# A transformer block on one core: the first loads in one queue in the order of need, the fourth q group behind k^T v, another priority table

## The chip, the cores and the metric

The kernel runs on one core of one Trainium2 chip. The metric is device time in microseconds (us) of that core, the median of several runs; less is better. One further execution was recorded by the hardware profiler, and all times of single instructions are from it.

The engines go by these names: PE is TensorE (matmuls; PEld its weight loads), DVE is VectorE, ACT is ScalarE, POOL is GpSimd, SP is SyncE. SP, ACT and POOL also start DMAs.

## The reference

The input x has 2048 rows (tokens) of 512, in bf16. Cut to what matters:

```python
phi = lambda t: jnp.where(t > 0, t + 1, jnp.exp(t)) + 1e-06

def A(x, wqkv, wo):                       # 32 heads of 16
    q, k, v = split(x @ wqkv)
    pq, pk = phi(q), phi(k)
    kv  = pk^T v                          # one 16x16 matrix for each head
    z   = sum of pk over the tokens
    o   = (pq @ kv) / (pq @ z + 1e-06)
    return o @ wo

def B(x, w_in, w_sp, b_sp, w_out):        # w_in 512x1792, w_sp 2048x2048, w_out 896x512
    z  = gelu(x @ w_in)
    z1 = z[..., :896]
    z2 = layernorm(z[..., 896:])
    g  = w_sp @ z2 + b_sp[:, None]        # mixes the tokens
    return (z1 * g) @ w_out

h  = x + A(layernorm(x), wqkv, wo)
h2 = h + B(layernorm(h), w_in, w_sp, b_sp, w_out)
```

Layer normalisation has no weights: it subtracts the mean of a row and divides by the root of the variance plus 1e-5.

## The kernel before

The 2048 rows are 16 tiles of 128 rows; two tiles are a pair, and four tiles (512 rows) are a group. Everything stays in on-chip memory from the first load to the last store.

**Stages.** (1) Each tile of x gets its statistics on DVE (L607, L611), ACT works out the reciprocal root (L621, L623), and DVE writes the normalised tile xn (L635). The statistics of several tiles share one pair of ACT instructions: the groups are 0, 1, 2-3, 4-7, 8-11, 12-15 (`LN1`). Four buffers hold xn. (2) xn is transposed to xT, either on TensorE (L673) with an ACT copy out of PSUM (L678), or by a DMA transpose that SP issues (L662); the constant `XDMA` says from which pair on DMA does it. (3) For each pair k and v are projected (L705: eight matmuls of 128x512 for k, eight for v). k goes through phi: Exp on ACT (L684) and two DVE instructions (L685, L692). v is copied by ACT (L719). (4) q is projected transposed, for each group in two halves of eight matmuls (L731), each with its phi. (5) k^T v is accumulated over all 16 tiles (L754, 64 narrow matmuls), masked to the heads and transposed on DVE (L766, L772, L774), and multiplied with wo (L784, L789, L792). (6) The denominators come from matmuls of q with the sums of k (`den`, L804; Ln and Exp on ACT, L808 and L811), are spread over the columns (`spread_den`, L821, L827) and scale q (`scale_pq`, L843, L847). (7) The scaled q times the product of stage 5 is added to x (L876, L881), and that is h. (8) h is normalised and transposed again, z2 (L904) and z1 (L949) are projected, and Gelu runs on ACT (L913, L954). (9) w_sp, which DMA transposes (L553) have brought in transposed, mixes the tokens (L979), and w_out projects the result (L997), which is stored.

**Order.** No engine's order is written by hand. `Program.op` records each operation with a cost and a priority; `schedule` then runs a list planner over the five engines. At each step it takes, on the engine that can start first, the candidate that can start at once (or within `PATIENCE`) with the lowest priority number. The order that comes out is fixed for each engine, and semaphore waits are put in for what an operation depends on. A dependency in `deps` becomes a wait; one in `after` only holds the planner back. The table `NUDGE` adds a number to each operation's priority, in the order in which operations are recorded. The planner counts 0.5 us of SP's time for a load, 1.3 us for a DMA transpose, and for the data of all loads one common wire of 340 GB/s.

**First loads.** SP issues x tile 0, the k weights in two halves, and seven pairs of x (x2 to x8, 256 KB each). ACT issues x tile 1 and the v weights; POOL issues the q weights, and later wo, w_in and w_out, each of which waits until POOL's DMA before it has landed. Behind its loads SP has the 16 DMA transposes for the first quarter of w_sp and ten for the second, with priority 5000, so that the transposes of xn go first wherever the planner has them ready.

**q groups.** `NQ1` says how many of the four q groups get priority `Q0 - 5 + gq` (75 and up). The others, none before the change, get `Q0 + Q3P` (88); k^T v has `Q0 + 2` (82).

```python
for gq in range(NQ1):
    for f in (0, 2):
        o = q_proj(gq, f, Q0 - 5 + gq)
load("pool", "wout", wout.all(), B_w_out.rearrange("(c p) f -> p c f", p=P), FH * D * 2).deps[o] = True
...
for gq in range(NQ1, NG):
    for f in (0, 2):
        q_proj(gq, f, Q0 + Q3P)
```

Of the kernel before, what the change touches and what calls it, by code (L numbers as in the profile page):

```python
# [10 lines left out]
P = 128  # L11
# [98 lines left out]
class Program:  # L110
# [13 lines left out]
    def op(self, eng, cost, fn, r=(), w=(), prio=None, after=(), dma=None, nbytes=0, lag=0.0):  # L124
        o = Op()
        o.eng, o.fn, o.cost, o.seq = eng, fn, cost, len(self.ops)
        o.prio = o.seq if prio is None else prio
        o.after, o.deps, o.tiles = list(after), {}, []
        o.marked, o.sem, o.semval, o.grp, o.bytes, o.lag = False, None, None, dma, nbytes, lag
        o.raw = set()  # L130
        for x in list(r) + list(w):
            t = getattr(x, "tile", None)
            if t is not None and t not in o.tiles:
                o.tiles.append(t)
                t.ops.append(o)
        rk = [k for x in r for k in x.keys]
        wk = [k for x in w for k in x.keys]
        for k in rk:
            p = self.writer.get(k)
            if p is not None:  # L140
                o.deps[p] = True
                o.raw.add(p)
        for k in wk:
            p = self.writer.get(k)
            if p is not None:
                o.deps[p] = True
                o.raw.add(p)
            for q in self.readers.get(k, ()):
                if q is not o:
                    o.deps[q] = True  # L150
        for k in rk:
            self.readers.setdefault(k, []).append(o)
        for k in wk:
            self.writer[k] = o
            self.readers[k] = []
        self.ops.append(o)
        return o
# [213 lines left out]

NUDGE = [
    0, 0, 0, 0, 0, 0, 0, 0, 0, 0, 0, 0, 0, 0, 0, 0, 0, 0, 0, 0, 0, 0, 0, 0, 0, 0, 0, 0, 0, 0, 0, 0, 0, 0, 0, 0,
    0, 0, 0, 0, 0, 0, 0, 0, 0, 0, 0, 0, 0, 0, 0, 0, 0, 0, 0, 0, 0, 0, 0, 0, 0, -24.5, 27.5, -1.5, 28, -65,
    396.5, 122.5, 93.5, 46, -45.5, -424.5, -26.5, -342, 3.5, 6.5, 17, -91, -52, -53.5, 190, -89, -15, 63.5,
    18.5, 5, -20, -57.5, -9, 143, 6.5, 0, -8, -3.5, 105.5, 89.5, 1122, -12, -84, 78.5, -154.5, 9, 512, -147.5,
    -5.5, -30.5, -26.5, 57, 2321.5, 66.5, 2453.5, 101, 2881.5, 445, 2436, -29.5, -0.5, 170.5, 126.5, 14.5, -4.5,
    -181.5, 53, -54, 0.5, 0, -1, -36.5, 79, 980, -17, 8, 29.5, 182.5, 0, 0, -61.5, 49, -72.5, -307.5, 112,
    191.5, -14, 0, -265, 0, -60.5, -64, 24, 154.5, -27, 112.5, 48, -217.5, 9, -9.5, 116, -88.5, 85.5, 182.5,
    -15.5, -45, 384, 113.5, 51.5, 69, 94.5, 14, 133.5, 521.5, 113.5, -157, 50.5, 391, -44.5, 116.5, -37, 404,  # L380
    274, 70.5, 62, -308, -114.5, 0, 366.5, 276.5, 195, 70.5, 61, -64, 53.5, -93, -104.5, -16, 0, -29, 0, 2, 9.5,
    40.5, 60.5, 133.5, 237, -64, -20, 173.5, 21, -26.5, -14.5, 26, 43, 655, 3377, 107.5, 92, 106, 226, 157,
    -173, 247.5, 64.5, 408.5, 11.5, -47, 85.5, -26, 112.5, 223.5, 8.5, -101.5, -48, -143.5, -44, -89, 0, 0,
    -141.5, -45, -54.5, 26, -11.5, -11.5, -364, 666, 25.5, -58, -73, -164, 0, 21.5, 0, 104.5, 73.5, 511.5, 151,
    258.5, 1, 1, 92, 51.5, 120, -98, 31, -100.5, 54, -130.5, 43, -2, -10.5, 34, 69.5, -53, 60.5, 11, -10.5,
    32.5, 295, 92.5, -9, 0, -83.5, 19.5, -118.5, 0, -10, 112, -15, -24.5, 5.5, 1.5, -119.5, -119.5, -54.5,
    -412.5, 83, -16.5, 72.5, 82, -46.5, 96.5, 944.5, 0, 55.5, 0, 300.5, -15, 745.5, 199.5, 311, 0, 147.5, -1,
    73, -49.5, -152, 12.5, 64.5, -567, 73.5, 15, 92.5, 136, 150.5, 7, 20, 126, 155.5, 807.5, -246, -154.5,
    -33.5, 1.5, 321, 14, 6, 99, 163, -11, 359, -28.5, -578.5, 0, -4.5, -371, -125.5, -205.5, -105, -58.5, -7, 0,
    448.5, 322, 6.5, 59, 5, 1, -1.5, 123.5, 45, 36.5, 36.5, -80, -8.5, 66, 10, 26, 1146.5, 186, 281.5, 31, 13,  # L390
    133, 13.5, -16.5, 67.5, 340, 428, 104, 213.5, -0.5, -1.5, 56, -261, -1.5, -1.5, 10, -63, -38.5, -28.5, -4,
    -6.5, -146.5, -342, 78.5, -66, 82.5, -333, -702, -291, 117.5, -20.5, 1205.5, 16, 54, 65, -31.5, -83.5,
    -68.5, -86.5, -178, -24, -279, -228.5, -63.5, -72.5, -44.5, 9.5, 75, 63.5, 157, -66.5, -47, 670.5, 83, 91.5,
    156.5, 458.5, -59, 218, 123, 39.5, 0, -53.5, 0, 98.5, -73.5, 60, -6, 33, -62, -73, -61.5, -4.5, 36.5, 183.5,
    -23.5, -11.5, 198, -21.5, 37, -173, -11.5, -49.5, -1, 130.5, 220.5, -7.5, -223.5, -16.5, -11, -20, -85.5,
    -21, 0, 5, -9.5, -18.5, -42.5, -80.5, -1.5, 20.5, -66.5, -62.5, 0.5, 1.5, 37.5, -10, 83.5, -614.5, -4.5,
    -567, 4, -52, 95, -286, -101.5, 27, 41.5, 13, 78, 241.5, -182.5, -39.5, 45.5, 7.5, 87.5, 3, -72.5, -124,
    -352, -11, -72, -9, -61, -104, 16.5, -210, 131.5, 36, 36.5, 49, -61.5, -14.5, 215, 186.5, -88.5, -113.5,
    -64.5, -116, 25, -3.5, 0, 0, 0, 0, -11, -220.5, -27, -76, -56.5, -89.5, -491, -21.5, 12, 75, 72.5, 123,
    31.5, 223.5, 27.5, 70, 41, -137, 252.5, 30, -259.5, 0, -16.5, -77, 35.5, 378,  # L400
]


# [1 line left out]
def bass_sequential_preLN__linear_attn_block__mixer_gmlp__prompt_kernel(  # L405
# [11 lines left out]
    _, S, D = A_x.shape  # L417
# [6 lines left out]
    VS = 136  # L424
    NP = NT // 2
    assert D == 512 and KD == 4 and NG == 4 and FH == KF * P and 512 < FH <= 1024
    WARM, XDMA, HDMA, LNACT = 8, 4, 1, 2
    WSP1 = 10
    DB, DC, SPP, PK, ZD = 6, 7, 8, 0.3, 2
    ONES, SCP, Q3P, NQ1 = 1, 7, 8, 4  # L430
    HC = P // DH
    EPS_PHI, EPS_DEN, EPS_LN = 1e-6, 1e-6, 1e-5

    x_dram, out_dram = A_x[0], out[0]
# [18 lines left out]
    x = View(s_x, 0, [NT, D], BF16)  # L453
    wq, wk, wv = [View(s_w3, i * KD * D * 2, [KD, D], BF16) for i in range(3)]
# [13 lines left out]
    zc = View(s_zc, 0, [KD, H], BF16)  # L468
# [55 lines left out]
    op = g.op  # L524
# [10 lines left out]
    def load(eng, name, dst, src, nbytes, prio=None, whole=False, after=()):  # L535
        return op(eng, 0.8 if eng == 'pool' else 0.5, lambda e: e.dma_start(dst.ap(), src), w=[dst], dma=(name, whole), nbytes=nbytes,
                  prio=prio, after=after)

    w3 = A_wqkv.rearrange("(c p) f -> p c f", p=P)
    load("sp", "x0", x[0, :], x_dram[0:P, :], P * D * 2)  # L540
    load("act", "x1", x[1, :], x_dram[P:2 * P, :], P * D * 2, prio=-20)
    for c in (0, 2):
        load("sp", "wk", wk[c:c + 2, :], w3[:, c:c + 2, D:2 * D], D * D, whole=True)
    for p in range(1, NP):
        load("sp", f"x{p + 1}", x[2 * p:2 * p + 2, :],
             x_dram[2 * p * P:(2 * p + 2) * P, :].rearrange("(n p) d -> p n d", p=P), 2 * P * D * 2)
        if p == 1:
            load("act", "wv", wv.all(), w3[:, :, 2 * D:3 * D], D * D * 2, prio=-19)

    def load_wsp(tg, sts, after=()):  # L550
        for st in sts:
# [26 lines left out]
                                              fill=0.0, base=DH, channel_multiplier=-1),  # L578
       r=[bmask.all()], w=[bmask.all()])

    load_wq = load("pool", "wq", wq.all(), w3[:, :, 0:D], D * D * 2)

    op("pool", 0.1, lambda e: e.memset(zc.all().ap(), 0.0), w=[zc.all()], after=[load_wq])
    op("pool", 0.5, lambda e: e.memset(sel.all().ap(), 0.0), w=[sel.all()])
    for c in range(KD):
        blk = sel.ap[H * c:H * (c + 1), c, :]
# [124 lines left out]
    for p in range(NP):  # L711
# [3 lines left out]
        if p == 6:  # L715
            load("pool", "win", win.all(), B_w_in.rearrange("(c p) f -> p c f", p=P), D * F * 2, after=[o])
        t = kv_proj(p, wv, 10 * p + 1)
        d = v[2 * p:2 * p + 2, :, 0:P]
        op("act", act_c(1024), lambda e, t=t, d=d: e.activation(  # L719
            d.ap(), flat(t().ap()).rearrange("p (n c f) -> p n c f", n=2, c=KD), ACT.Copy), r=[t()], w=[d],  # L720
           prio=10 * p + 1)
# [24 lines left out]
    for b in range(2):  # L746
        t = Tile(PS)
        for i in range(2):
            c = 2 * b + i
# [12 lines left out]
        d = zc[2 * b:2 * b + 2, 0:HC]  # L762
# [16 lines left out]
    for b in range(2):  # L779
        t = Tile(PS, 2)  # L780
        for i in range(2):
            c = 2 * b + i
# [4 lines left out]
        d = mw[2 * b:2 * b + 2, :]  # L787
        if b == 0:
            op("act", act_c(1024), lambda e, t=t, d=d: e.activation(d.ap(), t().ap(), ACT.Copy), r=[t()], w=[d],  # L789
               prio=Q0 + 3.5)  # L790
        else:
            op("dve", dve_c(1024), lambda e, t=t, d=d: e.tensor_copy(d.ap(), t().ap()), r=[t()], w=[d],  # L792
               prio=Q0 + 3.5)
# [72 lines left out]
    for u in UNITS:  # L866
# [13 lines left out]
        d = x[n0:n0 + k, :]  # L880
# [15 lines left out]
    for p in range(NP):  # L896
        transpose_pair(p, hn_t, hT, B0 + 10 * p + 4, p >= HDMA, ONES)
        for n in (2 * p, 2 * p + 1):
            t = Tile(PS, 2)
            l = hT[:, n * P:(n + 1) * P]  # L900
            for i, (a, b) in enumerate(((FH, FH + 512), (FH + 512, F))):
                def mm(e, t=t, i=i, a=a, b=b, l=l):
# [5 lines left out]
                   after=dens)  # L908
            d = gz2[n, :]
# [5 lines left out]
               after=last_lnexp)  # L915
            if by_act:
# [5 lines left out]
                   w=[q, u()], prio=pz + 1)  # L922
                op("pool", 0.25, lambda e, q=q: e.tensor_scalar(q.ap(), q.ap(), 1.0 / FH, None, op0=ALU.mult),
                   r=[q], w=[q], prio=pz + 1)
            else:
                for i, (a, b) in enumerate(((0, 512), (512, FH))):
                    s6, src = st_z[n, 6 * i:6 * i + 6], gz2[n, a:b]
                    op("dve", dve_c(b - a), lambda e, s6=s6, src=src: e.bn_stats(s6.ap(), src.ap()), r=[src], w=[s6],
                       prio=pz + 1)
                aggr(Row(st_z, n), 12, pz + 1)  # L930

    for gq in range(NG):
        rs = small([TPG], FP32)
        rstd_pow(st_z[gq * TPG:(gq + 1) * TPG, 13], rs.all(), B0 + 20 * gq + 43, TPG)
        for i in range(TPG):
            n = gq * TPG + i
# [135 lines left out]
```

## Time and profile before

| | us |
|---|---|
| median of 3 runs | 256.23 (256.05 to 256.33) |
| the profiled execution | 256.96 |
| its span, first to last instruction | 255.2 |
| PE busy | 242.6 |
| DVE busy | 139.0 |
| ACT busy | 83.1 |
| POOL busy | 26.0 |

The granted clock of TensorE is 1.0 throughout. The span starts with the first instruction; the rest of the execution's time lies around it. Idle time of an engine that is not the bottleneck costs nothing, and a wait in the tables is put down to what ended it.

### The profile page before, as it was taken

Reading aid. Unit: us, or ns where it says so; the run is one execution under the profiler, and the core shown is the slowest. Engines: PE = TensorE matmul, PEld = TensorE weight load, DVE = VectorE, ACT = ScalarE, POOL = GpSimd, SP = SyncE. Lnnn points to the kernel's source line nnn. Section 1 sums busy time; section 2 is a strip of 40 time slices with the busy share of each in tenths; the row PEclk is TensorE's granted clock in tenths of the full one; section 3 lists DMA queues with packets and bytes.
Section 4 is the critical chain, followed back from the end, with each engine's and each line's share of the span. In section 5 each row is a group of like instructions: output and inputs, shape, how many; then the busy total and the mean of one; then the engine's idle time right before and its main releaser. Section 6 shows DMA issues by size and latency. Waiting matters only on the chain.

```text
span 255.2 us, 3084 instructions
## 1 busy us (share of the span) xinstructions
PE 242.6 (95%) x1190; PEld 112.1 (44%) x1212; DVE 139.0 (54%) x265; ACT 83.1 (33%) x116; POOL 26.0 (10%) x66
## 2 busy tenths in 40 slices
PE   5879989999889999999999999999999999999995
PEld 1335434446334444444444444444444444444442
DVE  3498968957979998875212333333323333223443
ACT  3447565554992645878930000000010000000000
POOL 7310000001021331353200000000000000000000
PEclk9999999999999999999999999999999999999999
DMA  7999864474302314255444544101000010000022
GB/s 230 348 204 326 131 103 101 102 86 125 124 0 41 62 22 91 45 94 105 102 99 92 102 103 101 22 22 63 0 0 0 23 62 0 0 3 0 0 82 82
DMA packets 53310, 21.04 MB, mean 82 GB/s; under 512 B 47312, under 2 KB 52432, under 8 KB 53296
## 3 DMA queue, kind: packets, MB, share of 16 engines
q1 hardware_dynamic: 51824, 16.40, 30.7%
q0 software_dynamic: 800, 3.80, 4.3%
q10 hardware_dynamic: 672, 0.66, 0.7%
q8 instruction: 9, 0.15, 0.2%
q14 instruction: 5, 0.04, 0.1%
HBM read 7.47 MB, written 2.10 MB: 37 GB/s over the span
## 4 chain that ended last, share of the span: by engine, by line
PE 86%; DVE 5%; ACT 4%; POOL 1%; DMA 1%; issue 1%; POOLq 0%; ACTq 0%
PE ps L979 38%; PE ps L705 11%; PE ps L997 9%; PE ps L949 9%; PE ps L904 9%; PE ps L731 5%; PE ps L876 3%; PE ps L754 1%; DMA xT_pq_z<-xn 1%; DVE xT_pq_z L847 1%; DVE xn L635 1%; ACT xT_pq_z L678 1%; PE ps L673 1%; ACT wqkv_wsp L827 1%; DVE small L607 1%
## 5 line engine op out<-in xcount | busy, mean ns | idle before, releaser
L979 PE MATMUL ps<-wsp,pk_v_z 128*128 128x512 bf16 x328 | 72.8, 379 | 0.4
L985 DVE TENSOR_TENSOR r<-ps,e 128x512 bf16<-128x512 f32 x28 | 19.4, 692 | 71.1 <-PE ps L979 71.1
L979 PEld LDWEIGHTS ps<-wsp,pk_v_z 128*128 128x128 bf16 x336 | 32.9, 98 | 39.6
L705 PE MATMUL ps<-wqkv_wsp,xT_pq_z 128*128 128x512 bf16 x125 | 31.9, 406 | 3.5 <-ACT xT_pq_z L678 2.3
L954 ACT ACTIVATE xT_pq_z<-ps 128x1024 bf16<-128x1024 f32 x14 | 14.0, 1020 | 58.7 <-PE ps L949 58.6
L904 PE MATMUL ps<-win,hT 128*128 128x384 bf16 (+1 forms) x125 | 25.5, 352 | 0.5 <-ACT hT L678 0.3
L949 PE MATMUL ps<-hT,win 128*128 128x512 bf16 x109 | 25.3, 379 | 0.2
L607 DVE BATCH_NORM_STATS2 small<-xh 128x6 f32<-128x512 bf16 x32 | 21.2, 676 | 7.0 <-DMA xh<-in_A_x_dram 6.8
L997 PE MATMUL ps<-wout,xT_pq_z 128*128 128x512 bf16 x111 | 24.6, 379 | 0.1
L979 PE MATMUL ps<-wqkv_wsp,pk_v_z 128*128 128x512 bf16 x110 | 24.2, 379 | 0.1
L705 PEld LDWEIGHTS ps<-wqkv_wsp,xT_pq_z 128*128 128x128 bf16 x128 | 12.9, 103 | 21.0 <-issue 4.9
L684 ACT ACTIVATE e<-ps 128x1024 bf16<-128x1024 f32 x16 | 16.3, 1024 | 10.3 <-PE ps L731 4.8
L913 ACT ACTIVATE pk_v_z<-ps 128x896 bf16<-128x896 f32 x16 | 14.4, 915 | 13.8 <-PE ps L904 13.8
L904 PEld LDWEIGHTS ps<-win,hT 128*128 128x128 bf16 x128 | 12.4, 98 | 12.9 <-ACT hT L678 0.6
L1003 DVE TENSOR_TENSOR r<-ps,xh 128x512 bf16<-128x512 f32 x16 | 11.1, 692 | 11.7 <-PE ps L997 11.7
L997 PEld LDWEIGHTS ps<-wout,xT_pq_z 128*128 128x128 bf16 x112 | 10.9, 98 | 13.2
L979 PEld LDWEIGHTS ps<-wqkv_wsp,pk_v_z 128*128 128x128 bf16 x112 | 10.9, 98 | 13.2
L876 PE MATMUL ps<-pk_v_z,xT_pq_z 128*128 128x512 bf16 x64 | 15.6, 379 | 1.1 <-ACT pk_v_z L913 0.6
L949 PEld LDWEIGHTS ps<-hT,win 128*128 128x128 bf16 x112 | 11.0, 98 | 12.6
L731 PE MATMUL ps<-xT_pq_z,wqkv_wsp 128*128 128x512 bf16 x63 | 15.2, 379 | 0.1
L635 DVE TENSOR_SCALAR xn<-xh,small 128x512 bf16<-128x512 bf16 x32 | 12.1, 405 | 4.6 <-DMA xT_pq_z<-xn 2.2
L988 DVE TENSOR_TENSOR xT_pq_z<-xT_pq_z,r 128x512 bf16<-128x512 bf16 x28 | 11.9, 425 | 1.0
(69 smaller groups left out, 175.4 us busy)
## 6 DMA issues: line engine op xcount, KB each, us to landing
out_dram<-r SPq DMA_DIRECT2D x16, 128.0 KB, 1.7
xh<-in_A_x_dram SPq DMA_DIRECT2D x7, 256.0 KB, 8.4
win<-in_B_w_in_dram POOLq DMA_DIRECT2D x1, 1792.0 KB, 8.3
wout<-in_B_w_out_dram POOLq DMA_DIRECT2D x1, 896.0 KB, 7.3
wsp<-in_B_w_sp_dram SPq DMA_TRANSPOSE x48, 2.7
wqkv_wsp<-in_A_wqkv_dram ACTq DMA_DIRECT2D x1, 512.0 KB, 7.1
wqkv_wsp<-in_A_wqkv_dram SPq DMA_DIRECT2D x2, 256.0 KB, 4.7
wqkv_wsp<-in_A_wqkv_dram POOLq DMA_DIRECT2D x1, 512.0 KB, 8.4
```

The source lines that it names most:

```text
L607: op("dve", dve_c(512), lambda e: e.bn_stats(s6.ap(), src.ap()), r=[src], w=[s6], prio=prio)
L635: return op("dve", 0.2 + 0.00026 * n, lambda e: e.tensor_scalar(dst.ap(), src.ap(), m.ap(), rs.ap(), op0=ALU.subtract, op1=ALU.mult), r=[s ...
L684: op("act", act_c(1024), lambda e: e.activation(e_().ap(), t(flat).ap(), ACT.Exp), r=[t()], w=[e_()], prio=prio)
L705: i = e.matmul(t(bank(ti)).ap(), lhsT=lhs.ap()[:, c, :], rhs=rhs.ap()[:, c, :], start=(c == 0), stop=(c == KD - 1))
L731: r_ = e.matmul(t(bank(i)).ap(), lhsT=lhs.ap()[:, c, :], rhs=rhs.ap()[:, c, :], start=(c == 0), stop=(c == KD - 1))
L876: i = e.matmul(t(bank(ti)).ap(), lhsT=l.ap()[:, c, :], rhs=mw[c, :].ap(), start=(c == 0), stop=(c == KD - 1))
L904: k = e.matmul(t(bank(i)).ap()[:, 0:b - a], lhsT=l.ap()[:, c, :], rhs=win[c, a:b].ap(), start=(c == 0), stop=(c == KD - 1))
L913: op("act", act_c(FH, ptr=by_act), lambda e, t=t, d=d, acc={"accum_out": m.ap()} if by_act else {}: e.activation(d.ap(), t(flat).ap()[:, 0 ...
L949: k = e.matmul(t(bank(i)).ap(), lhsT=l.ap()[:, c, :], rhs=r_.ap()[:, c, :], start=(c == 0), stop=(c == KD - 1))
L979: k = e.matmul(t(bank(0)).ap(), lhsT=l.ap()[:, s - a, :], rhs=r_.ap()[:, s - a, :], start=(s == 0), stop=(s == NT - 1))
L985: op("dve", dve_c(512), lambda e: e.tensor_tensor(gb().ap(), t(bank(0)).ap(), bsp().ap()[:, tg * GW:(tg + 1) * GW], ALU.add), r=[t(), bsp( ...
L997: k = e.matmul(t(bank(0)).ap(), lhsT=l.ap()[:, fc, :], rhs=wout[fc, :].ap(), start=(fc == 0), stop=(fc == KF - 1))
```

## The change

The v weights move from ACT's queue to SP's, behind x3 (the pair of tiles 4 and 5). The q weights move from POOL's queue to SP's, behind the last x load. The loads get priorities of their own in that order: x0, two halves of the k weights, x2, x3, v weights, x4 to x8, q weights. For the planner alone, the first half of the k weights counts 170000 bytes more. On POOL, the `zc` memset is no longer held back behind the load of the q weights.

`XDMA` goes from 4 to 3: pair 3 is transposed by DMA and no longer on TensorE. `NQ1` goes from 4 to 3: the fourth q group is recorded after the operations of stage 5 and gets priority 88 in place of 78; with that, the load of w_out depends on the third group's phi in place of the fourth's.

The table `NUDGE` is replaced. Its first 61 entries (loads, constants, warm-up) stay 0. Some sums of base and entry in the new table: k^T v 163 to 170; the second halves of the fourth group's two projections 107.5 and 105, the first halves 956 and 510.5.

```diff
 NUDGE = [
     0, 0, 0, ...
-    ..., -24.5, 27.5, -1.5, 28, -65,
+    ..., -207, 57, -273, -167.5, 0, 49,
...
-    WARM, XDMA, HDMA, LNACT = 8, 4, 1, 2
+    WARM, XDMA, HDMA, LNACT = 8, 3, 1, 2
+    WV = 2
...
-    ONES, SCP, Q3P, NQ1 = 1, 7, 8, 4
+    ONES, SCP, Q3P, NQ1 = 1, 7, 8, 3
...
-    load("sp", "x0", x[0, :], x_dram[0:P, :], P * D * 2)
+    load("sp", "x0", x[0, :], x_dram[0:P, :], P * D * 2, prio=0)
     load("act", "x1", x[1, :], x_dram[P:2 * P, :], P * D * 2, prio=-20)
     for c in (0, 2):
-        load("sp", "wk", wk[c:c + 2, :], w3[:, c:c + 2, D:2 * D], D * D, whole=True)
+        load("sp", "wk", wk[c:c + 2, :], w3[:, c:c + 2, D:2 * D], D * D + (170000 if c == 0 else 0), whole=True, prio=c / 2 + 1)
+
+    def load_x(p, prio):
+        load("sp", f"x{p + 1}", x[2 * p:2 * p + 2, :],
+             x_dram[2 * p * P:(2 * p + 2) * P, :].rearrange("(n p) d -> p n d", p=P), 2 * P * D * 2, prio=prio)
+
     for p in range(1, NP):
-        load("sp", f"x{p + 1}", x[2 * p:2 * p + 2, :],
-             x_dram[2 * p * P:(2 * p + 2) * P, :].rearrange("(n p) d -> p n d", p=P), 2 * P * D * 2)
-        if p == 1:
-            load("act", "wv", wv.all(), w3[:, :, 2 * D:3 * D], D * D * 2, prio=-19)
+        load_x(p, 2 + p)
+    load("sp", "wv", wv.all(), w3[:, :, 2 * D:3 * D], D * D * 2, prio=2.5 + WV)
+    load("sp", "wq", wq.all(), w3[:, :, 0:D], D * D * 2, prio=2 + NP)
...
-    load_wq = load("pool", "wq", wq.all(), w3[:, :, 0:D], D * D * 2)
-
-    op("pool", 0.1, lambda e: e.memset(zc.all().ap(), 0.0), w=[zc.all()], after=[load_wq])
+
+    op("pool", 0.1, lambda e: e.memset(zc.all().ap(), 0.0), w=[zc.all()])
```

## The prediction, made before the changed kernel was run

> **What bounds the kernel now.** I read the page's shares first, then its chain, then a table by stage, then the timeline of the stages where TensorE idles.
>
> ```profile
> PE 242.6 (95%) x1190; PEld 112.1 (44%) x1212; DVE 139.0 (54%) x265; ACT 83.1 (33%) x116; POOL 26.0 (10%) x66
> PE 86%; DVE 5%; ACT 4%; POOL 1%; DMA 1%; issue 1%; POOLq 0%; ACTq 0%
> ```
>
> TensorE is busy 242.6 of 255.2 us and carries 86% of the chain, so the time is TensorE's work plus its holes. The change touches little of the work; it can only close or open holes. The table by stage (columns: stretch, its length, busy time of PE, PEld, DVE, ACT, POOL, granted clock, DMA share, GB/s) says where they are:
>
> ```profile
> 7.89:16.30 8.41, 6.83 (x25) 2.70 (x25) 6.42 (x18) 3.46 (x5) 1.27 (x3) 1.00 1.28 273
> 16.30:34.70 18.40, 18.28 (x94) 8.57 (x96) 15.83 (x33) 11.80 (x16) 0.75 (x1) 1.00 0.91 214
> 34.70:41.50 6.80, 5.62 (x24) 2.16 (x26) 4.20 (x8) 3.21 (x5) 0.00 (x0) 1.00 0.61 100
> 57.02:60.85 3.83, 3.79 (x65) 3.61 (x63) 2.46 (x6) 1.02 (x1) 0.59 (x1) 1.00 0.15 34
> 60.85:77.48 16.63, 13.97 (x91) 5.69 (x93) 14.48 (x29) 14.96 (x21) 1.64 (x3) 1.00 0.31 93
> 77.48:129.70 52.22, 51.95 (x252) 25.16 (x258) 38.08 (x82) 34.14 (x52) 15.72 (x36) 1.00 0.35 70
> ```
>
> Three holes can be reached: 1.58 us in the first stretch, 1.18 us (6.80 less 5.62) from 34.70, 2.66 us (16.63 less 13.97) from 60.85. After 77.48 TensorE is full to the last matmul, so a microsecond saved before that is saved at the end, as long as nothing new waits there.
>
> The first hole in the timeline (start, length, what, idle before and its releaser):
>
> ```profile
> 9.10 1.29 DVE L607 BATCH_NORM_STATS2 small<-xh 128x6 f32<-128x512 bf16 x2 [2.58 <-DMA xh<-in_A_x_dram]
> 7.89 6.38 PE L705 MATMUL ps<-wqkv_wsp,xT_pq_z 128*128 128x512 bf16 x16 [0.69 <-ACT xT_pq_z L678]
> 14.10 0.61 PE L673 MATMUL ps<-small,xn 128*128 128x128 bf16 x8
> 16.30 3.63 PE L705 MATMUL ps<-wqkv_wsp,xT_pq_z 128*128 128x512 bf16 x15 [1.58 <-ACT xT_pq_z L678]
> ```
>
> Pair 1 of x lands at 9.10, its normalised tiles are ready at 12.76 (DVE: 11.96 plus 0.80), by when k and v of pair 0 are already queued ahead; its transposes follow them at 14.10, and nothing covers the ACT copy after that: 1.58 us idle.
>
> The second hole, by SyncE's queue:
>
> ```profile
> 2.21 5.49 SPq L536 DMA_DIRECT2D xh<-in_A_x_dram  x7
> 7.75 25.09 SPq L553 DMA_TRANSPOSE wsp<-in_B_w_sp_dram  x16
> 32.88 5.19 SPq L662 DMA_TRANSPOSE xT_pq_z<-xn  x4
> ```
>
> Tiles 8 to 11 are normalised by 28.95 (27.57 plus 1.38), but SyncE is inside sixteen w_sp transposes of 1.57 us (25.09/16) until 32.84; TensorE runs dry at 34.70 and the chain waits on these transposes to 38.96. The planner counts 1.3 us for one and 0.5 for a load, so SyncE falls behind its plan as the w_sp transposes add up.
>
> **Order of the first loads.** From 2 to 13 us the three queues together move 338 GB/s, 3.72 MB, which is all of x and of the q, k, v weights (3.67 MB): the wires are full and the total cannot shrink. Only the order can. In the new order the bytes up to pair 1 are 0.13+0.13+0.52+0.26 = 1.05 MB, at 338 GB/s there by 5.1 us (the shortest landing in the trace, 2.5 us, from an issue at 2.2 gives 4.7), against 9.10. Up to the v weights it is 1.84 MB, 7.4 us; v matmuls start after the eight of k, at 7.89+3.2 = 11.1, so a v load 3 us late still costs nothing. The q weights end at 12.9; the first q matmul is at 19.76. Pool's wo load no longer waits for them and may start some 3 us earlier, against the last x tiles, which DVE reads only late (its tile statistics run until 25 us).
>
> DVE is busy with tiles 0 and 1 until 6.51. From there the old length from statistics to normalised (12.76 less 9.10, 3.66) gives 10.2, inside k of pair 0. So pair 1's transposes can run before or among v of pair 0, whose matmuls (0.40 us each at this point) then cover the 1.02 us copy. Worth 0 (order unchanged) to 1.58; I take 1.3, because ACT also owes the 1.02 us Exp of k there.
>
> The Trainium skill (DMA: Bandwidth & Descriptors, "Issuing engines are not separate DMA queues") says that DMAs started from several engines share the same 16 engines, and that several issuers save only sequencer time. The 338 GB/s over three queues agrees; by that rule the merge itself buys no bandwidth and costs SyncE the issues.
>
> **That cost.** wv leaves ACT (0.46, followed by idling until 5.11: no gain), wq leaves POOL (0.99, off the path), and SyncE gets two more issues, bounded by the trace's shortest and longest plain ones, 0.39 and 1.28 us each; I take 0.46, the weights' own rows: 0.92. Everything behind on SyncE moves: the w_sp transposes (needed from 129.7) and, among them, the transposes of xn.
>
> **Pair 3 by DMA (XDMA 4 to 3).** It removes eight TensorE transposes, 0.056 each by the group of twelve in 0.67 us: 0.45 us off TensorE, and a 1.02 us ACT copy. It adds two DMA transposes of 1.26 on SyncE ahead of tile 8's. With N w_sp transposes ahead, tile 8 is issued at 7.75+0.92+1.57N+2.52 and lands 2.6 later (35.5 less 32.88). TensorE would get there at 34.70-1.3-0.45 = 32.9. N=12 lands at 32.6, no wait; N=14 at 35.8, the old time; N=15 at 37.3; N=16 at 38.9. Which N? Today 16 fit between 5.0 and 25.8 by the planner's own costs. The first loads now end at 6.0, 2.6 go to tiles 6 and 7, and tile 8 should be ready some 2 us sooner: (23.8-6.0-2.6)/1.3 is 11.7. So 12: the hole of 1.18 shrinks. Later tiles meet the same lag, so I take 0.5 off (range 1.18 gained to 1.75 spent, which is all that was won ahead; beyond N=14 more is lost).
>
> **Fourth q group.** Moved: 16 matmuls (16 times 0.216 = 3.46 us), two Exp (1.02) and on DVE two pairs of 0.43 and 1.22. Today its last phi runs on DVE from 58.28 to 59.97, hidden under k^T v (57.02 to 60.82). The new priorities: k^T v 163 to 170 (base 82), second halves of the two q pairs 107.5 and 105, first halves 956 and 510.5 (lower goes first). So half of it, 1.73 us, can still precede k^T v and cover the last v eviction as now; the other half is filler for the 2.66 us of holes behind. But DVE (14.48 of 16.63 busy) and ACT (14.96) are nearly full there. If the 3.3 us of DVE work slot into DVE's 2.15 idle, the stretch ends 59.1+14.48+3.3 = 76.9, 0.6 gained; with all of the group behind, 57.4+17.8 = 75.2, 2.3 gained; with half behind and nothing overlapped, 59.1+16.63+3.3 = 79.0, 1.5 lost. I take 0.4 gained, near the overlapped half. What needs group 3 has room: its denominator matmuls ran at 62.4, the first z matmul (planned behind them) at 70.5. The wout and b_sp loads move too; both are used only after 129.
>
> The rest of the table reorders a stretch where TensorE idles 0.27 of 52 us: between 0.27 gained and, for a new wait, one hole as long as the longest that TensorE shows anywhere, 1.58, lost; I take 0, since other engines idle there.
>
> **Sum.** 1.3+0.45+0.5+0.4 = 2.65. The profiled execution took 256.96 (span 255.2 plus 1.8 around it) and would take 254.3. It ran 0.73 above the median of 256.23, so the median becomes 253.6.
>
> **Rivals.** A difference under 0.2%, 0.5 us, is no change here.
>
> (a) SyncE's queue takes over and it is slower: with N=15 or more, tile 8 lands 1.8 us later than now whatever was won before; less 0.4 from the q group that is 257.6. It decides from N=14. For it: the two issues and two transposes put 3.4 us ahead, and SyncE already runs late. Against: tile 8 should be ready sooner. Chance 0.17. This is where the skill's rule on issuers above would show.
>
> (b) The q group behind k^T v loads DVE where it is full: 1.5 lost instead of 0.4 gained gives 255.5, in the band 254.7 to 256.8. For it: DVE and ACT at 87 and 90%. Chance 0.20 (faster 0.10, same 0.05, slower 0.05).
>
> (c) The loads land in the new order, but TensorE's order around pair 0 stays, or the group in effect stays ahead of k^T v: only the 0.45 remains, 255.8. For it: the second halves' priority. Chance 0.13 (faster 0.05, same 0.05, slower 0.03).
>
> The forecast has 0.50; its own range is 251.6 to 255.4: above, the first and second holes give nothing (1.8); below, two thirds of the way to every gain at its bound (1.58+0.45+1.18+2.3+0.27 = 5.8, 250.4). Together: faster 0.65, same 0.10, slower 0.25. The range runs from 251.6 to (a)'s 257.6 and leaves out (a) with N=16 and the largest gains.
>
> **What would show it.** Right: first pair-1 statistics near 6.5 instead of 9.10; no 1.58 us hole before the second L705 group, which starts near 15; TensorE past tile 8's matmuls by about 33; 24 instead of 32 transposes at L673 in the first 30 us; PE busy above 14.5 of 16.6 behind k^T v. Wrong: fifteen or more w_sp transposes ahead of tile 8 on SyncE, TensorE waiting for xT longer than 1.2 us in sum, DVE releasing TensorE for more than 3 us behind k^T v, or new holes between 78 and 130.

## The result, and the profile after

The changed kernel takes 253.04 us in the median of four runs (252.97 to 253.29), the kernel before 256.14 in the runs beside it (255.30 to 256.33). The ratio is 0.9887, with a 95% interval of 0.9864 to 0.9910: 3.1 us faster. The profiled execution took 253.07 (span 251.3), so between the two profiles there are 3.9 us, more than between the medians. Executions that took clearly longer than the others of the same kernel do not count in any ratio; one of them is the profiled one of the reversed experiment below (898.8 us), whose median is given without it and which has no usable trace.

The page of the changed kernel, its shares and its chain (most line numbers behind L are three higher than in the kernel before; L553, which issues the w_sp transposes, is L557 now):

```profile
PE 240.3 (96%) x1204; PEld 110.7 (44%) x1204; DVE 137.4 (55%) x265; ACT 82.1 (33%) x115; POOL 24.5 (10%) x65
PE 84%; DVE 6%; DMA 5%; SPq 2%; ACT 1%; issue 1%
```

TensorE still sets the end, but DMA and SyncE's queue now stand in the chain with 7%. Where they come in, the timeline of TensorE shows (start, length, what, count, and in brackets the idle time before and its releaser):

```profile
7.66 2.99 PE L708 MATMUL ps<-wqkv_wsp,xT_pq_z 128*128 128x512 bf16 x12 [0.29 <-ACT xT_pq_z L681]
10.49 0.62 PE L676 MATMUL ps<-small,xn 128*128 128x128 bf16 x8
12.23 2.76 PE L708 MATMUL ps<-wqkv_wsp,xT_pq_z 128*128 128x512 bf16 x12 [0.25 <-ACT xT_pq_z L681]
16.64 2.75 PE L734 MATMUL ps<-xT_pq_z,wqkv_wsp 128*128 128x512 bf16 x12 [1.65 <-DMA wqkv_wsp<-in_A_wqkv_dram]
25.34 1.02 PE L708 MATMUL ps<-wqkv_wsp,xT_pq_z 128*128 128x512 bf16 x4 [0.33 <-DMA xT_pq_z<-xn]
35.17 1.02 PE L734 MATMUL ps<-xT_pq_z,wqkv_wsp 128*128 128x512 bf16 x4 [0.71 <-DVE xT_pq_z L695]
52.43 3.79 PE L757 MATMUL ps<-pk_v_z 128*128 128x130 bf16 x64
56.06 1.03 PE L734 MATMUL ps<-xT_pq_z,wqkv_wsp 128*128 128x512 bf16 x4
57.35 1.04 PE L734 MATMUL ps<-xT_pq_z,wqkv_wsp 128*128 128x512 bf16 x4
```

Pair 1's transposes (L676, at 10.49) now stand inside v of pair 0, and the next projection starts at 12.23 with a hole of 0.25 in place of 1.58. But three other things are in these lines. The first twelve matmuls took 0.25 us each, with a short wait for the v weights among them, where the kernel before shows 0.40 for its first sixteen. TensorE then waits 1.65 us for the q weights. And eight matmuls of the fourth q group run behind k^T v (L757), eight in front of it.

VectorE's first statistics of pair 1, 9.10 before:

```profile
7.35 1.29 DVE L610 BATCH_NORM_STATS2 small<-xh 128x6 f32<-128x512 bf16 x2 [0.43 <-DMA xh<-in_A_x_dram]
```

SyncE's queue of the changed kernel:

```profile
7.41 0.47 SPq L536 DMA_DIRECT2D wqkv_wsp<-in_A_wqkv_dram  x1
7.93 14.68 SPq L557 DMA_TRANSPOSE wsp<-in_B_w_sp_dram  x9
22.65 2.57 SPq L665 DMA_TRANSPOSE xT_pq_z<-xn  x2
25.26 3.36 SPq L557 DMA_TRANSPOSE wsp<-in_B_w_sp_dram  x2
28.67 5.19 SPq L665 DMA_TRANSPOSE xT_pq_z<-xn  x4
```

Tile 8's transposes are issued at 28.67 behind 9+2 = 11 w_sp transposes; before, at 32.88 behind 16. The table by stage (stretch, length, busy time of PE, PEld, DVE, ACT, POOL, clock, DMA share, GB/s):

```profile
56.06:77.00 20.94, 19.20 (x120) 8.26 (x118) 19.11 (x35) 15.46 (x21) 1.30 (x2) 1.00 0.53 125
77.00:126.70 49.70, 49.70 (x246) 23.88 (x244) 34.06 (x79) 34.64 (x52) 15.06 (x36) 1.00 0.32 65
```

Behind k^T v TensorE idles 1.74 us (20.94 less 19.20), against 2.66; after 77 it is full, as before.

k^T v is a good dividing line. It starts at 57.02 before and at 52.43 after, 4.59 earlier. The stretches up to it, first of the kernel before and then of the changed one:

```profile
0.00:57.02 57.02, 50.83 (x229) 22.24 (x233) 41.60 (x78) 30.90 (x41) 8.07 (x27) 1.00 0.82 182
0.00:52.43 52.43, 46.02 (x216) 19.93 (x217) 39.65 (x76) 28.88 (x39) 8.12 (x27) 1.00 0.73 172
```

Of the 4.59, 1.73 us is q work that now comes later and 0.45 the transposes of pair 3. The other 2.41 us is not less waiting: up to k^T v TensorE idles 6.19 us before (57.02 less 50.83) and 6.41 after. It is TensorE's busy time, 2.63 less besides the 1.73 and the 0.45, which is about what the slow first matmuls of the one profile come to (sixteen of them at 0.40 instead of 0.25 us are 2.4). What these matmuls are worth in the median, only the experiments can tell. From k^T v's start to the end of the span it is 198.2 us before and 198.9 after; with 1.73 more work in it, 1.04 was saved there. 2.41+0.45+1.04 is the 3.9 between the profiles.

### The profile page after: what moved, and what is told of

It is laid out like the page before. It is cut to its first block, busy times and chain, and to the rows that moved or that the text cites. A ratio compares the mean times of both kernels' runs of the same rounds, so it can differ in the third digit from the quotient of the medians.

```text
span 251.3 us, 3084 instructions
## 1 busy us (share of the span) xinstructions
PE 240.3 (96%) x1204; PEld 110.7 (44%) x1204; DVE 137.4 (55%) x265; ACT 82.1 (33%) x115; POOL 24.5 (10%) x65
## 4 chain that ended last, share of the span: by engine, by line
PE 84%; DVE 6%; DMA 5%; SPq 2%; ACT 1%; issue 1%
PE ps L982 38%; PE ps L907 10%; PE ps L1000 10%; PE ps L952 10%; PE ps L708 6%; PE ps L734 5%; PE ps L879 4%; DMA wqkv_wsp<-in_A_wqkv_dram 4%; SPq L536 2%; DVE xT_pq_z L695 2%; PE ps L757 1%; DVE xT_pq_z L850 1%; DMA xT_pq_z<-xn 1%; ACT e L687 1%; DVE small L610 1%
## 5 line engine op out<-in xcount | busy, mean ns | idle before, releaser
L708 PE MATMUL ps<-wqkv_wsp,xT_pq_z 128*128 128x512 bf16 x128 | 29.3, 379 | 0.9 <-ACT xT_pq_z L681 0.5
L907 PE MATMUL ps<-win,hT 128*128 128x512 bf16 (+1 forms) x128 | 25.7, 353 | 0.4 <-ACT hT L681 0.4
L708 PEld LDWEIGHTS ps<-wqkv_wsp,xT_pq_z 128*128 128x128 bf16 x128 | 12.1, 98 | 16.5 <-ACT xT_pq_z L681 1.2
L931 DVE BATCH_NORM_STATS2 small<-pk_v_z 128x6 f32<-128x512 bf16 (+1 forms) x16 | 9.8, 619 | 9.6 <-ACT pk_v_z L916 9.4
```

The source lines that it names most:

```text
L708: i = e.matmul(t(bank(ti)).ap(), lhsT=lhs.ap()[:, c, :], rhs=rhs.ap()[:, c, :], start=(c == 0), stop=(c == KD - 1))
L907: k = e.matmul(t(bank(i)).ap()[:, 0:b - a], lhsT=l.ap()[:, c, :], rhs=win[c, a:b].ap(), start=(c == 0), stop=(c == KD - 1))
```

## The experiments

In all of them the orders are held: the planner may take only the next operation of a list, one list for each engine, that was written out from its own plan of the kernel before or of the changed kernel. Each edit then changes what it names and no other order (where the loads move, a few constants on POOL move with them).

```python
+                    if o.seq != PIN[e][len(order[e])]:
+                        continue
```

Each time is a median of several executions, and each ratio, with its 95% interval, is to executions of the kernel before beside them on the same chip; their medians were 256.33, 256.57 and 256.42. Line numbers in the traces are shifted by the lists (some 50 for most).

**A longer warm-up, to take the slow matmuls out.** `WARM` from 8 to 14, in both kernels.

> The kernel before with its orders held, 14 instead of 8 warm-up matmuls, so that TensorE is busy without a gap from 1.4 us to its first real work. Question: how much of the 3.1 us between the two kernels is that TensorE ran its first 16 matmuls at 0.40 us each in the one profile and at 0.22 in the other. If the clock is the cause: k and v of pair 0 run at 0.22, pair 1 then waits for its data, the projection of pair 1 starts near 14.5 instead of 16.3, and the time falls by 1.5 to 1.8 us, to about 254.5. If only the loads and the order matter: 256.1, or up to 0.5 more for the longer warm-up.

> The changed kernel with its orders held, 14 instead of 8 warm-up matmuls. If its first matmuls run at full rate anyway: 253.0, the longer warm-up hidden by the wait for the q weights at 15 to 16.6 us. If the clock is the cause of the gain, the pair of kernels with 14 warm-up matmuls differs by about 1.4 us instead of 3.1; if the loads and the order are, by about 3.

Measured: the kernel before with it 257.86 (ratio 1.0040, 1.0000 to 1.0081), not faster; the changed one 252.88 (0.9840, 0.9774 to 0.9907), as without. TensorE of the first:

```profile
8.44 3.63 PE L755 MATMUL ps<-wqkv_wsp,xT_pq_z 128*128 128x512 bf16 x16 [0.47 <-ACT xT_pq_z L728]
14.09 3.63 PE L755 MATMUL ps<-wqkv_wsp,xT_pq_z 128*128 128x512 bf16 x15 [1.58 <-ACT xT_pq_z L728]
35.51 3.15 PE L755 MATMUL ps<-wqkv_wsp,xT_pq_z 128*128 128x512 bf16 x7 [3.02 <-DMA xT_pq_z<-xn]
38.87 3.20 PE L755 MATMUL ps<-wqkv_wsp,xT_pq_z 128*128 128x512 bf16 x8 [0.22 <-DMA xT_pq_z<-xn]
```

and its SyncE queue:

```profile
6.41 26.37 SPq L603 DMA_TRANSPOSE wsp<-in_B_w_sp_dram  x16
32.83 5.33 SPq L712 DMA_TRANSPOSE xT_pq_z<-xn  x4
```

The sixteen matmuls ran at full pace and the next projection started at 14.09, 2.2 us earlier. Nothing of it reached the end: TensorE waits 3.02 us for tile 8, which lands at 35.5 as ever. So in the kernel before everything won ahead of 35.5 is lost there, and the second hole's 1.18 us in the profile was only what was left of it in an execution whose first matmuls were slow.

The wait also cost more than its own length. In the table by stage, the stretch from 34.7 us (the clock is the third number from the end):

```profile
34.70:41.50 6.80, 5.78 (x14) 2.18 (x16) 3.21 (x6) 1.02 (x1) 0.00 (x0) 0.50 0.56 99
```

While TensorE waited, its granted clock fell to 0.50 and stayed there until 41.5. The fifteen matmuls behind the wait took from 35.51 to 41.91, where the kernel before took from 35.56 to 39.47, and k^T v started at 59.18 instead of 57.02. That is why this execution took 259.12, longer than the kernel before. Of the ten executions, the two whose mean granted clock was 1.00 took 256.02 and 256.31, as the kernel before; the others, with a mean of 0.985 to 0.993, took 257.23 us and more.

**The place in SyncE's queue alone.** In the kernel before, tiles 8 to 11 go behind 13 w_sp transposes and tiles 12 to 15 behind 15; loads, table and all other engines stay. In the second kernel the warm-up is longer as well.

```python
-sp: x loads, 16 w_sp, tiles 8 9 11 10, 1 w_sp, tiles 15 14 13 12, 9 w_sp
+sp: x loads, 13 w_sp, tiles 8 9 11 10, 2 w_sp, tiles 15 14 13 12, 11 w_sp
```

> The kernel before, all orders held but SyncE's: the transposes of tiles 8 to 11 go behind 13 w_sp transposes instead of 16, those of tiles 12 to 15 behind 15 instead of 17. Nothing else changes. If SyncE's queue is what holds TensorE at 35.5 us, tile 8 lands near 31 instead of 35.5 and the second hole (1.2 us, or more where the clock came early) closes: 254.6 to 255.4. If the loads or the table are needed: 256.0 to 256.5.

> The same with 14 warm-up matmuls, which alone brought nothing because all that it won early was lost at 35.5 us (3.0 us of waiting for tile 8). If that wait is the queue's and nothing else is next late: 252.6 to 253.8, the time of the changed kernel without its loads and without its table. If another wait takes its place: 255 or more.

Measured: 253.21 (0.9879, 0.9853 to 0.9905), a larger gain than was expected, and with the warm-up 252.96 (0.9874, 0.9855 to 0.9894), as expected. TensorE of the first kernel, and its SyncE queue:

```profile
31.11 5.34 PE L755 MATMUL ps<-wqkv_wsp,xT_pq_z 128*128 128x512 bf16 x24
53.56 3.79 PE L804 MATMUL ps<-pk_v_z 128*128 128x130 bf16 x64
```

```profile
5.87 22.10 SPq L603 DMA_TRANSPOSE wsp<-in_B_w_sp_dram  x13
28.02 5.19 SPq L712 DMA_TRANSPOSE xT_pq_z<-xn  x4
```

Tile 8 is issued at 28.02 and TensorE runs through from 31.11 without a wait. Moving a few w_sp transposes behind the xn transposes, and nothing else, wins as much as the whole change. Among the executions with a mean granted clock of 1.00 the medians are 255.87 for the kernel before and 253.06 with the queue moved: 2.8 of the 3.2 us are there without a fall of the clock.

**The reverse in the changed kernel.** Tiles 8 to 11 behind 16 instead of 11.

```python
-sp: loads, 9 w_sp, tiles 6 7, 2 w_sp, tiles 8 9 11 10, 5 w_sp, ...
+sp: loads, 9 w_sp, tiles 6 7, 7 w_sp, tiles 8 9 11 10, ...
```

> The changed kernel, all orders held but SyncE's: the transposes of tiles 8 to 11 go behind all 16 first w_sp transposes, as in the kernel before, instead of 11. By the prediction's formula each of the five costs 1.3 to 1.6 us: tile 8 is issued near 35.5 instead of 28.7, lands near 38 instead of 31.2, and TensorE, which wants it at 31.7, waits some 6 us: 257.5 to 260. If the place in the queue is not the cause: under 255.

Measured: 260.56 in the median (1.0176, 1.0148 to 1.0205), 7.5 us more than the changed kernel and above the range. So the place in the queue is the cause, but the wait alone, worked out at some 6 us, does not fill the 7.5. The mean granted clock was 0.980 to 0.987 in these executions, so slow matmuls behind the wait, as in the run with the longer warm-up, are the likely rest; no trace of this kernel shows them.

**The loads alone, and everything but the loads.** First the kernel before with the new loads; then the changed kernel with the old three queues.

```python
# before_loads: the kernel before with
+    load("sp", "wv", wv.all(), ..., prio=2.5 + WV)     # behind x3
+    load("sp", "wq", wq.all(), ..., prio=2 + NP)       # behind x8
# after_oldloads: the changed kernel with
+    load("act", "wv", wv.all(), ..., prio=-19)
+    load_wq = load("pool", "wq", wq.all(), ...)        # wo waits for it again
```

> The kernel before with every engine's order held (only the loads themselves move), but the first loads in one queue as in the change. Theory one, from the kernel before with the longer warm-up: whatever is won early is given back at 35.5 us, where TensorE waits for the transposes of tile 8 behind sixteen w_sp transposes, and those start later by two issues: 256.5 to 257.2. Theory two, the prediction's first term: the load order itself is worth 1.3: 254.5 to 255.2.

> The changed kernel with its orders held, but the first loads in three queues as before (v weights from ACT, q weights from POOL). If the order of the loads is what closes the first hole: pair 1 lands near 9.1 again, TensorE waits for its transposes in the middle of v of pair 0, the projection of pair 1 starts 2 us later (near 14.5 instead of 12.2), and the wait for the q weights (1.65) goes: 253.5 to 254.5. If the new order of the engines alone brings the gain: 252.5 to 253.2.

Measured: the first 260.01 (1.0152, 1.0100 to 1.0203), the second 250.75 (0.9766, 0.9710 to 0.9822). Both lie outside what was expected, the first above and the second below, and both say that the new loads cost time: 3.4 us in the old order and 2.3 in the new one (253.04 less 250.75). TensorE and SyncE of the kernel before with the new loads:

```profile
36.96 4.99 PE L759 MATMUL ps<-wqkv_wsp,xT_pq_z 128*128 128x512 bf16 x15 [5.13 <-DMA xT_pq_z<-xn]
```

```profile
7.79 26.44 SPq L608 DMA_TRANSPOSE wsp<-in_B_w_sp_dram  x16
34.27 5.25 SPq L716 DMA_TRANSPOSE xT_pq_z<-xn  x4
```

and of the changed kernel with the old loads:

```profile
12.20 0.72 PE L724 MATMUL ps<-small,xn 128*128 128x128 bf16 x8 [1.60 <-DVE xn L686]
16.63 2.75 PE L782 MATMUL ps<-xT_pq_z,wqkv_wsp 128*128 128x512 bf16 x12
50.75 3.79 PE L805 MATMUL ps<-pk_v_z 128*128 128x130 bf16 x64
```

```profile
7.10 13.83 SPq L603 DMA_TRANSPOSE wsp<-in_B_w_sp_dram  x9
26.21 5.85 SPq L713 DMA_TRANSPOSE xT_pq_z<-xn  x4
```

With the old loads pair 1 comes late again and TensorE waits 1.60 us for it, as the prediction's first term says. But the q weights are there, the transposes of tile 8 are issued at 26.21 instead of 28.67, none of the waits at 16, 25 and 35 us is left, and k^T v starts 1.7 us sooner. In the kernel before, the new loads bring tile 8 out at 34.27 instead of 32.88. The time of the two issues does not explain that by itself: the sixteen w_sp transposes start at 7.79 against 7.75 and take 26.44 us against 25.09. TensorE's wait there is 5.13 us, and again the granted clock falls to 0.50 in it (from 36.4 to 39.8); part of the 3.4 us is that.

**wo behind the q weights.** The wait that POOL's wo load had before the change is put back, by a dependency.

```python
-                load("pool", "wo", wo.all(), ..., after=[o])
+                load("pool", "wo", wo.all(), ..., after=[o]).deps[load_wq] = True
```

> The changed kernel, orders the same, with one wait more: POOL's load of wo starts only when the q weights have landed, as it did before the change. Theory one: wo shares the wires with the q weights and makes them late, and TensorE's 1.65 us wait for them at 15.0 us closes wholly or mostly: 251.5 to 252.3. Theory two: the q weights are held by the x loads and w_sp transposes, or DVE is next late by the same amount: 252.8 to 253.2.

Measured: 251.84 (0.9801, 0.9745 to 0.9858). TensorE:

```profile
16.04 2.75 PE L784 MATMUL ps<-xT_pq_z,wqkv_wsp 128*128 128x512 bf16 x12
25.36 0.81 PE L758 MATMUL ps<-wqkv_wsp,xT_pq_z 128*128 128x512 bf16 x3 [0.94 <-DMA xT_pq_z<-xn]
```

wo is issued at 15.55, when the q weights have landed; in the changed kernel they landed at 16.51. The wait for them is gone, though the matmuls ahead of it came later in this execution; a part returns at 25.36, where pair 3's DMA transposes are late.

**Pair 3 back on TensorE.** `XDMA` 4, the two transposes out of SyncE's list, the eight matmuls and the copy put behind pair 2's k.

> The changed kernel, orders held but for pair 3, which TensorE transposes again (XDMA 4): eight transposes and one ACT copy more, two DMA transposes on SyncE less ahead of tile 8. By the prediction's second term TensorE's 0.45 us come back: 253.3 to 253.6. If the waits for the transposes of pair 3 (0.33 and some 0.1 us at 25 us) cost as much as the transposes: 252.8 to 253.2.

Measured: 253.35 (0.9881, 0.9852 to 0.9911), within the interval of the change itself. Its new hole:

```profile
26.70 0.81 PE L754 MATMUL ps<-wqkv_wsp,xT_pq_z 128*128 128x512 bf16 x3 [1.34 <-ACT small L670]
```

The transposes end at 25.35 and ACT copies at once, from 25.39 to 26.41, but where the pair was put no matmul is left to cover the copy. That costs more than the waits that it spares. The 0.45 us is neither shown nor refuted.

**The first projection of the fourth q group ahead of k^T v.** Its matmuls and its phi are moved in front of the second's.

> The changed kernel, orders held but for the first projection of the fourth q group, which goes ahead of k^T v again together with its phi. By the prediction's fourth term its eight matmuls leave the holes behind k^T v empty: the stretch from k^T v on has more idle TensorE, 253.3 to 253.7. By the rival, VectorE and ScalarE get relief where they are full: 252.0 to 252.8. No effect: 252.9 to 253.2.

Measured: 252.84 (0.9862, 0.9834 to 0.9891), no effect that these runs can tell. The stretch behind k^T v, by stage, with it:

```profile
57.40:77.00 19.60, 17.06 (x108) 7.77 (x112) 17.94 (x33) 15.05 (x21) 1.30 (x2) 1.00 0.39 98
```

TensorE idles 2.54 us there, against 1.74 with the eight matmuls behind. But from k^T v to the end the span takes 197.3 (250.9 less 53.61); with 1.73 of work added, 199.0 against the change's 198.9. The filler closes 0.8 us of holes behind k^T v and wins about 0.15 in all, since the stretch gets longer with it.

**Two attempts at a better version.** In the three-queue version of the changed kernel, once the v weights are issued behind ACT's table load and the q weights later on POOL; and once pair 1 of x goes ahead of the k weights.

> The changed kernel's orders with the loads in three queues as before the change, but the v weights issued behind ACT's table load and the q weights 2.5 to 4 us later on POOL, so that pair 1 of x meets less traffic and SyncE still has two issues less. If the 1.6 us wait for pair 1's normalised tiles in the three-queue version closes with nothing new: 249.0 to 249.9. If pair 1 is no earlier: 250.6 to 251. If the v or q weights come late: over 251.

> The changed kernel's orders with the first loads in three queues as before the change, and pair 1 of x issued ahead of the k weights. If pair 1 lands 0.8 to 1 us earlier and the k weights stay in time: the wait of 1.6 us for pair 1's normalised tiles shrinks and the time is 249.7 to 250.4. If the k weights are late by as much: 250.6 to 251.5.

Measured: 251.49 (0.9812, 0.9771 to 0.9852) and 251.81 (0.9828, 0.9781 to 0.9875), with single times from 250.55 to 252.82; neither can be told from the 250.75 of the plain three queues.

In the profile of the first, TensorE's wait for pair 1 shrinks from 1.60 to 0.93, and a wait of 0.56 for DVE appears at 33; in that of the second, with pair 1 first, TensorE waits 0.61 for the k weights. The changed kernel with the old loads has the lowest median of this study.

## Why the prediction was right, and for which reasons

The number, 253.6 against 253.04, holds, and so does the frame: all of it was won ahead of 77 us, where TensorE has holes. That the sum of 2.65 came close to the 3.1 is luck all the same: its two largest errors, one of them in sign, nearly cancelled.

**First loads, 1.3 won: wrong sign.** The mechanism up to 12 us is as described: pair 1 lands earlier (its statistics start at 7.35, where 6.5 had been expected), its transposes go into v of pair 0, and the hole of 1.58 becomes 0.25. What the step missed is behind it. It put the q weights at 12.9 and their first use at 19.76, the use of the old order. The new order uses them at 15.0, and they came at 16.5. The step saw that wo would start earlier, but set it against the last x tiles only; wo was issued at 7.42, beside the q weights, and putting its wait back takes the hole away. And it priced the two more loads on SyncE at 0.92; the tile 8 transposes came 1.4 us later in the old order (34.27 against 32.88) and 2.5 in the new one (28.67 against 26.21), because the w_sp transposes ahead of them went more slowly too. Over all, the loads cost 3.4 and 2.3 us. The sentence from the Trainium skill (DMA: Bandwidth & Descriptors, "Issuing engines are not separate DMA queues") pointed this way: with the loads merged 328 GB/s were moved from 2 to 13 us, with three queues 338, so the merge bought no bandwidth.

**SyncE's queue, 0.5 won: far too small.** The formula for tile 8 was right: for the 11 w_sp transposes that are ahead of it now it gives 28.46, and 28.67 was measured. Twelve had been expected, and no wait is left for tile 8. But the gain was capped at the 1.18 us of holes in the profile. The hole is the difference between two times, TensorE's arrival and SyncE's delivery, and the profile caught TensorE late, with sixteen matmuls at 0.40 us. With those at full pace the same hole is 3.0, and moving three transposes in the queue wins 3.2 in the median. This one term is as large as the whole change. In the two traces with a wait of 3 us or more the matmuls behind it were slow as well, for which the prediction had no term.

**Pair 3 by DMA, 0.45:** TensorE's eight transposes are gone, and 0.33 us and a little more came back as a wait at 25 us; the experiment could not resolve the rest.

**The fourth q group, 0.4:** half of it went behind k^T v, as the priorities suggested, though as the first whole projection and not as the first half of both. It is worth about 0.15.

**The rest of the table, taken as nothing:** of the 1.04 us won behind k^T v some 0.9 remain when the q group's 0.15 is taken off. The other reordering there is what is left to explain them; no experiment took it apart.

**The rivals.** (a) is real: its mechanism is what the kernel before suffers from, what the reversed experiment shows at 260.6, and it decides where the prediction put it, by the number of transposes ahead. The change simply moves that number the other way. (b) did not show. (c) is false for the first part, and half true for the q group.

## What to carry to other kernels

When an engine waits for a queue that runs at its own pace, the hole in one profile is not the value of that wait. Work out when the queue delivers and when the engine could arrive at best; until the delivery moves, nothing won ahead of it counts, as the longer warm-up showed. After a long wait, look at the granted clock of the matmuls behind it, too. And when loads are put in the order of need, take the need from the new order, and count what the queue that receives them has to deliver next.

## What the runs showed of the hardware

The first real matmuls ran at 0.40 us each up to 13.4 us in one profile, at 0.22 from 7.66 in another and between the two in others (4.21 us for twelve, 5.32 for sixteen), behind the same eight warm-up matmuls. The granted clock column shows this only in part: it says 0.50 from 7.6 to 11.0 us in the profile with the 5.32, but 1.00 all through the slow matmuls of the kernel before. The Trainium skill (TensorE: Matmul & The Clock Gate, Part 1) says that the clock is released after a window of activity that runs freely, so that the transition varies; the spread here agrees with it. Fourteen warm-up matmuls had TensorE at full pace from the first real matmul in all three profiles that were taken with them.

The granted clock fell to 0.50 in both traces in which TensorE waits 3 us or more: 2.2 us after the last matmul in a wait of 3.02 us, where it came back 6.8 us later, and 4.5 us after it in a wait of 5.13, where it came back after 3.4. Between 12 us and k^T v, no other usable profile shows a longer wait of TensorE than 1.65 us, and in none of them does the column fall there.

The sixteen w_sp transposes ended at 32.84 when they began at 7.75 and at 32.78 when they began at 6.41, 1.57 and 1.65 us each, while later ones took 1.28 (33.25, two in 2.56). They do not go at one pace. In the kernel before, single ones took 2.65 us at 7.7 and 1.93 at 10.4, then 1.26 from 13.7 to 17.6, up to 2.52 between 18.9 and 26, and 1.26 again from 29. So something other than SyncE's issue sets their pace in the slow stretches. The first loads, and w_in, which POOL issues at 17.78, share the wires then and are the likely cause; no run took them away.
